# Seven products of quarters for the second matrix product of the last two token groups, with the activations' sums on GpSimd and on VectorE

## The chip, the cores and the metric

The kernel runs on one core of one Trainium2 chip. A core has TensorE (PE, which multiplies matrices from SBUF into PSUM), VectorE (DVE), ScalarE (ACT), GpSimd (POOL), and SyncE (SP), from whose queue most DMA transfers start. Each engine works through its own instructions in their order and waits on semaphores for the others. The metric is the device time of one execution in microseconds (us), lower is better.

## The reference

Attention in a causal window, then a two-layer MLP over its output:

```python
batch, n_heads, seq, head_dim = (8, 8, 576, 64)        # window = 128
scores = scale * np.matmul(q, k.transpose(0, 1, 3, 2))
scores = np.where(mask, scores + bias[None], -1000000000.0)   # mask: 0 <= rel < window
scores = scores - np.max(scores, axis=-1, keepdims=True)
attn = np.exp(scores)
attn = attn / (np.sum(attn, axis=-1, keepdims=True) + 1e-09)
attn_out = np.matmul(attn, v)
...
n_tokens, d_model, d_ff = (4608, 512, 2048)
x = attn_out.transpose(0, 2, 1, 3).reshape(B * S, H * D)
h = x @ w_in
g = h * (1.0 / (1.0 + np.exp(-h)))
return g @ w_out
```

## The kernel before

The 4608 tokens are nine groups of 512 (`NG` = 9, `TG` = 512), and the 2048 hidden columns are 16 blocks of 128 (`NF`). A *step* n = 16 g + f is group g with hidden block f: group 7 is steps 112 to 127, group 8 is steps 128 to 143. Every step has a first product (`gemm1`, line 650) into a PSUM bank `h`, an activation in four instructions, and a second product (`gemm2`, line 719) that adds into four PSUM banks `o` (tags w, x, y, z), one for each 128 tokens of the group.

From group 2 (first product) and 3 (second) on, all operands are float16 and each number is a high part and a low remainder; a product is high x high, high x low and low x high. So a step has 12 matmuls in the first product, 4 parts of the 512 inputs times 3, and 12 in the second, 4 tiles of tokens times 3, each of which moves 512 columns. In group 2 the first product has the same columns in 24 matmuls of 256.

The activation of a step: `act1` is a tanh on ScalarE from PSUM (line 666); `act2` on VectorE makes gt = (tanh + 1) h, with h from PSUM (671); `act3` on ScalarE rounds gt to the high part gh (681); `act4` on VectorE takes the remainder gl (687).

Attention for the later tokens runs among the MLP steps. It goes in 72 half blocks p: scores on TensorE (439), the bias with the row maximum on VectorE (469, four instructions), exp on ScalarE (479), a float16 high part on ScalarE (488) and remainder on VectorE (493), two DMA transposes, attention times v on TensorE (543), a division on VectorE (561, 562, 570) and a split of the result (580, 142). Ahead of a half block the float16 parts of q and k are made (385 on ScalarE, 391 on VectorE), and those of v once for two half blocks (415 on GpSimd, 421 on VectorE).

The order is written out by hand. The loop goes through positions, four for each step (two halves of `gemm1`, two halves of the `gemm2` of the step before), and a table `plan` says which other pieces are issued ahead of each position; within one position a small `rank` sorts them. An engine then runs what it was issued in that order. In group 7 a half block of attention falls on every second step: the scores stand ahead of the first product of an odd step, attention times v ahead of that of an even one. The last half block is issued before the end of group 7, and group 8 has no attention.

At the end of a group the second product of the last step follows at once on that of the step before it, so the activation of the last step has only one second product to hide behind.

## Time and profile before

| | |
|---|---|
| median of 3 runs | 926.47 us (925.91 to 926.49) |
| the profiled execution | 926.23 us, of which the traced span is 924.4 us |
| TensorE busy | 914.6 us (99%), granted clock 1.0 |
| VectorE / ScalarE / GpSimd busy | 645.0 / 559.6 / 116.0 us |
| group 7 (744.01 to 837.42 us of the span) | 93.41 us |
| group 8 up to the end of its matmuls (837.42 to 920.33 us) | 82.91 us |

In the rows of the profile a line number is that of the kernel before. `out<-in` are the program's names, `xN` counts instructions, and a time in brackets is how long the engine had been idle before the instruction, with what released it. Rows of the timeline give start and duration in us; a busy TensorE may still be a TensorE that overlaps the ends of its matmuls, so the pace of matmuls is read from their starts.

### The profile page before, as it was taken

The page shows a single profiled execution, that of the slowest core. Times are in us where ns is not written, and L with a number is a line of the kernel's source. Part 1 is how long each engine was busy: PE and PEld are TensorE (multiplying, and loading weights), DVE is VectorE, ACT ScalarE, POOL GpSimd, SP SyncE. Part 2 cuts the span into 40 slices and gives each one's busy share as a digit, 9 for nine tenths or more (in the row PEclk, how much of TensorE's full clock was granted, in tenths as well). Part 3 has the DMA queues.
Part 4 walks back from the last instruction along what each step waited for, and adds up shares of the span by engine and source line. Part 5 has one row for each costly group of instructions (what it writes and reads, how often), then busy time and mean ns, then how long its engine had stood idle before and what let it go on. Part 6 is the DMA issues. An engine that isn't in the chain of part 4 may idle for free.

```text
span 924.4 us, 17093 instructions
## 1 busy us (share of the span) xinstructions
PE 914.6 (99%) x6426; PEld 572.4 (62%) x6426; DVE 645.0 (70%) x1629; ACT 559.6 (61%) x1149; POOL 116.0 (13%) x115
## 2 busy tenths in 40 slices
PE   9999999999999999999999999999999999999998
PEld 8867777777787886555555555555555555544443
DVE  6889876446776778888788778666867777743222
ACT  7778997675556764666677755555655565533222
POOL 2343442222221220000000000000000000000000
PEclk9999999999999999999999999999999999999999
DMA  8977825243275645434598736444545454211001
GB/s 311 392 189 225 256 57 129 69 91 80 71 218 152 178 115 137 114 94 112 114 247 219 203 88 163 112 103 104 160 115 115 114 160 113 65 35 52 1 1 45
DMA packets 197747, 122.89 MB, mean 133 GB/s; under 512 B 166432, under 2 KB 166816, under 8 KB 197664
## 3 DMA queue, kind: packets, MB, share of 16 engines
q1 hardware_dynamic: 197376, 121.54, 49.3%
q8 instruction: 50, 0.82, 0.4%
q14 instruction: 33, 0.27, 0.1%
q10 hardware_dynamic: 288, 0.26, 0.1%
HBM read 71.96 MB, written 9.44 MB: 88 GB/s over the span
## 4 chain that ended last, share of the span: by engine, by line
PE 85%; DVE 5%; ACT 1%; issue 1%; ACTq 0%
PE o L719 38%; PE h L650 29%; PE h L655 8%; PE av L543 4%; PE sp L439 3%; PE sp L446 2%; DVE gt L671 1%; DVE hr L493 1%; DVE t L469 0%; DVE w L816 0%; DVE vmx L204 0%; ACT t L479 0%; DVE x L142 0%; ACT w L804 0%; DVE wr L810 0%
## 5 line engine op out<-in xcount | busy, mean ns | idle before, releaser
L719 PE MATMUL o<-w,gh 128*128 128x512 f16 (+1 forms) x1152 | 351.2, 386 | 0.0
L650 PE MATMUL h<-xt,w 128*128 128x512 f16 (+1 forms) x1536 | 310.5, 353 | 0.0
L650 PEld LDWEIGHTS <-w 128*128 128x128 f16 x1536 | 144.6, 98 | 125.8 <-issue 2.2
L666 ACT ACTIVATE gt<-h,gsc 128x512 f32<-128x512 f32 x112 | 77.0, 687 | 239.8 <-PE h L650 237.7
L719 PE MATMUL o<-w,gl 128*128 128x512 f16 (+1 forms) x576 | 221.6, 385 | 0.2 <-DVE gl L142 0.2
L671 DVE SCALAR_TENSOR_TENSOR gt<-gt,h 128x512 f32<-128x512 f32 x144 | 98.7, 686 | 147.3 <-ACT gt L666 146.8
L719 PEld LDWEIGHTS <-gh 128*128 128x128 f16 x768 | 74.8, 98 | 89.1
L479 ACT ACTIVATE t<-t,mx 128x256 f32<-128x256 f32 (+1 forms) x288 | 125.2, 486 | 5.2 <-DVE mx L469 5.0
L493 DVE SCALAR_TENSOR_TENSOR hr<-t,hr 128x512 f16<-128x512 f32 (+1 forms) x128 | 89.3, 703 | 29.7 <-ACT hr L488 29.6
L687 DVE SCALAR_TENSOR_TENSOR gl<-gt,gh 128x512 f16<-128x512 f32 x96 | 66.8, 696 | 42.4 <-ACT gh L681 41.3
L655 PE MATMUL h<-xh,w 128*128 128x512 f32 x256 | 89.8, 405 | 0.0
L719 PEld LDWEIGHTS o<-w,gh 128*128 128x128 f32 x384 | 69.8, 188 | 15.3 <-DVE vsc L264 0.3
L415 POOL TENSOR_SCALAR v<-rv,vsc 128x512 f16<-128x512 f32 x30 | 25.2, 841 | 427.8 <-DMA rv<-v 351.8
L681 ACT ACTIVATE gh<-gt 128x512 f16<-128x512 f32 x96 | 60.4, 629 | 28.1 <-DVE gt L671 23.7
L488 ACT ACTIVATE hr<-t 128x512 f16<-128x512 f32 (+1 forms) x128 | 71.4, 595 | 1.4 <-DVE hr L493 1.4
L719 PEld LDWEIGHTS <-gl 128*128 128x128 f16 x384 | 37.6, 98 | 46.2 <-DVE gl L687 1.2
L543 PEld LDWEIGHTS <-hl 128*128 128x128 f16 x1464 | 51.4, 98 | 16.5 <-issue 5.2
L469 DVE CUSTOM_DVE_ANT_0 t<-sp,tab,vsc 128x256 f32<-128x256 f32 (+1 forms) x144 | 58.5, 461 | 1.8 <-PE sp L439 1.4
L140 POOL TENSOR_TENSOR gl<-gt,gh 128x512 fp32r<-128x512 f32 x30 | 38.6, 1286 | 164.2 <-ACT gh L679 148.9
L543 PE MATMUL av<-v,hl 128*128 128x65 f16 (+1 forms) x1464 | 54.8, 193 | 1.6 <-DVE mx L469 1.5
L655 PEld LDWEIGHTS h<-xh,w 128*128 128x128 f32 x256 | 48.1, 188 | 12.3 <-issue 0.2
L469 DVE CUSTOM_DVE_ANT_0 t<-sp,tab 128x256 f32<-128x256 f32 (+1 forms) x144 | 50.1, 402 | 3.3 <-PE sp L446 2.9
(135 smaller groups left out, 1006.5 us busy)
## 6 DMA issues: line engine op xcount, KB each, us to landing
r<-qk SPq DMA_DIRECT2D x36, 512.0 KB, 3.9
qs<-qk SPq DMA_DIRECT2D x18, 512.0 KB, 5.1
out<-ot SPq DMA_DIRECT2D x35, 256.0 KB, 2.4
wr<-w_in SPq DMA_DIRECT2D x16, 512.0 KB, 6.7
wr<-w_out SPq DMA_DIRECT2D x16, 512.0 KB, 6.2
rv<-v SPq DMA_DIRECT2D x30, 256.0 KB, 4.0
vm<-v SPq DMA_DIRECT2D x27, 256.0 KB, 5.0
q<-qk SPq DMA_DIRECT2D x18, 256.0 KB, 3.3
```

Source lines behind the costliest of these rows:

```text
L469: nc.vector.tensor_tensor_reduce(out=st[p]["t"][u][:, h, 2 * P - n :], in0=st[p]["sp"][h][:, u, o].rearrange("p o c -> p (o c)"), in1=tab[ ...
L479: nc.scalar.activation(x, x, AF.Exp, bias=st[p]["mx"][:, 2 * u + h : 2 * u + h + 1], scale=-1.0)
L488: nc.scalar.activation(split_of(p, u, hr)[:, 0], t[:, :, 2 * P - n :], AF.Copy, scale=PSCALE)
L493: nc.vector.scalar_tensor_tensor(out=hr[:, 1], in0=t[:, :, 2 * P - n :], scalar=PSCALE, in1=hr[:, 0], op0=ALU.mult, op1=ALU.subtract)
L543: nc.tensor.matmul(av[:, 2 * u + h, : rhs.shape[-1]], lhs, rhs, start=(n == 0), stop=(n == len(seq) - 1), skip_group_check=True,)
L650: nc.tensor.matmul(o, w[:, wp, cc], x, start=start and k == 0, stop=stop, skip_group_check=True)
L655: nc.tensor.matmul(hps[n], w[:, cc], x, start=(half == 0 and i == 0), stop=(half == 1 and i == len(seq) - 1), skip_group_check=True,)
L666: nc.scalar.activation(gt, hps[n], AF.Tanh, scale=scale)
L671: nc.vector.scalar_tensor_tensor(out=gt, in0=gt, scalar=1.0, in1=hps[n], op0=ALU.add, op1=ALU.mult)
L681: nc.scalar.activation(gh, gt, AF.Copy, scale=CUT)
L687: nc.vector.scalar_tensor_tensor(out=gl, in0=gt, scalar=CUT, in1=gh, op0=ALU.mult, op1=ALU.subtract)
L719: nc.tensor.matmul(ops[ti], a[:, t], w, start=(f == 0 and i == 0), stop=(f == NF - 1 and i == len(seq) - 1), skip_group_check=True,)
```

## The change

Groups 7 and 8 (`FAST`) take a second product by quarters, seven instead of eight. A is the activation of 256 tokens (two tiles of 128) by two hidden blocks, j and j + 8; B is `w_out` of these two hidden blocks by two halves of 256 output columns. The seven products are (A11+A22)(B11+B22), (A21+A22)B11, A11(B12-B22), A22(B21-B11), (A11+A12)B22, (A21-A11)(B11+B12) and (A12-A22)(B21+B22); each moves 256 columns, again in three matmuls, and they are summed over j = 0 to 7 in halves of the banks w, x, y, z. Steps are renumbered within a group: the first eight are the first 256 tokens, the next eight the other 256, and a step's first product makes two hidden blocks for 256 tokens in 24 matmuls of 256 columns.

- `act_sums` makes the five sums of quarters of gt (two, two and one quarter, in three instructions), on GpSimd in group 7, on VectorE in group 8. `act3` and `act4` then work on seven quarters (one instruction of five, one of two) in place of four. In group 7 `act3` and `act4` are issued one position later than before.
- The float16 parts of the five sums of `w_out` are made in steps 80 to 111 (groups 5 and 6), for one j in every 16 positions (`SUM_WORK`): seven additions or subtractions and three instructions for remainders on GpSimd, four copies on ScalarE.
- v's high part moves from GpSimd to ScalarE in groups 7 and 8.
- After eight steps the seven products are joined on ScalarE (one instruction) and VectorE (six) and stored from there, three stores on SP's queue and one on ScalarE's. Behind a join the second product of the first step is issued one step later, so that it follows two first products.
- The very last step has its second product in the plain way, in quarters that are added and stored one by one.

On VectorE, at steps 116 to 118, before (t, mx: row maximum of half block 68; q16, k16: remainders for block 34; hr: remainder of the weights; r, xs: division; the rows `mx68` alone are left out):

```order
L671 SCALAR_TENSOR_TENSOR gt116_9778<-gt116_9778,h116_9757 128x512
L687 SCALAR_TENSOR_TENSOR gl116_9792<-gt116_9778,gh116_9791 128x512
L142 SCALAR_TENSOR_TENSOR x33_9795<-xs66_9767,x33_9795 128x256
L469 ISA t68_0_9831,mx68_9822<-sp68_0_9804,tab_65,vsc3_6995 128x256
...
L671 SCALAR_TENSOR_TENSOR gt117_9845<-gt117_9845,h117_9824 128x512
L391 SCALAR_TENSOR_TENSOR q16_69_9781<-r16_69_9636,vsc3_6995,q16_69_9781 64x512
L687 SCALAR_TENSOR_TENSOR gl117_9858<-gt117_9845,gh117_9857 128x512
L391 SCALAR_TENSOR_TENSOR k16_34_9679<-r16_69_9636,vsc3_6995,k16_34_9679 128x512
L493 SCALAR_TENSOR_TENSOR hr68_0_9863<-t68_0_9831,hr68_0_9863 128x512
...
L493 SCALAR_TENSOR_TENSOR hr68_1_9900<-t68_1_9833,hr68_1_9900 128x512
L671 SCALAR_TENSOR_TENSOR gt118_9923<-gt118_9923,h118_9902 128x512
```

and after:

```order
L763 SCALAR_TENSOR_TENSOR gt116_10026<-gt116_10026,h116_9991 128x512
L147 SCALAR_TENSOR_TENSOR x33_10048<-xs66_10007,x33_10048 128x256
L799 SCALAR_TENSOR_TENSOR gl116_10061<-gt116_10026,gh116_10060 128x640
L799 SCALAR_TENSOR_TENSOR gl116_10061<-gt116_10026,gh116_10060 128x256
L480 ISA t68_0_10099,mx68_10082<-sp68_0_10064,tab_65,vsc3_6996 128x256
...
L763 SCALAR_TENSOR_TENSOR gt117_10119<-gt117_10119,h117_10084 128x512
L399 SCALAR_TENSOR_TENSOR q16_69_10032<-r16_69_9839,vsc3_6996,q16_69_10032 64x512
L399 SCALAR_TENSOR_TENSOR k16_34_9889<-r16_69_9839,vsc3_6996,k16_34_9889 128x512
L504 SCALAR_TENSOR_TENSOR hr68_0_10142<-t68_0_10099,hr68_0_10142 128x512
...
L799 SCALAR_TENSOR_TENSOR gl117_10155<-gt117_10119,gh117_10154 128x640
L799 SCALAR_TENSOR_TENSOR gl117_10155<-gt117_10119,gh117_10154 128x256
L504 SCALAR_TENSOR_TENSOR hr68_1_10186<-t68_1_10101,hr68_1_10186 128x512
```

The remainder gl of the even step still stands ahead of the row maximum; that of the odd step now stands behind q16, k16, the first hr and the division. The three sums of each step stand on GpSimd, between gt here and gh on ScalarE.

On ScalarE, at the join in the middle of group 7 (step 120), after; `once` is the part of the join that ScalarE makes, `of` what is stored:

```order
L759 ACTIVATE gt120_10421<-h120_10386,gsc7_9586 128x512
L393 ACTIVATE q16_71_10427<-r16_71_10231,vsc3_6996 128x512
L884 ACTIVATE once7_0_10443<-m7_0_1_9798,gsc7_9586 128x512
L591 CAST x34_10447<-xs68_10402 128x256
L876 DMA out<-of7_0_0_10441 128x256
L784 ACTIVATE gh120_10467<-gt120_10421 128x640
L784 ACTIVATE gh120_10467<-gt120_10421 128x256
L393 ACTIVATE k16_35_10282<-r16_71_10231,vsc3_6996 128x512
L759 ACTIVATE gt121_10526<-h121_10491,gsc7_9586 128x512
```

The store's DMA stands ahead of gh of step 120 and of the tanh of step 121; before, there was no store at this place.

The diff, cut to its core:

```diff
+FAST = (NG - 2, NG - 1)
+HALF_F = NF // 2
+SUMS, SUMS_STEP = 320, 16
...
     def v_hi(i):
         rv = rvs[i]
+        if pos[0] // (SLICE * NF) in FAST:
+            nc.scalar.activation(v1[:, i % VSLOTS, :, 0:D], rv, AF.Copy, scale=vsc[i // NBLK][:, 0:1])
+            return
...
+    def sum_float(j, k):
+        if k == 0:
+            wsum["r"] = pool.tile([P, 2, DM], F32, tag="big", name=f"wr{j}")
+        w = w16[1, j + k * HALF_F]
+        nc.gpsimd.tensor_add(wsum["r"][:, k], w[:, 0], w[:, 1])
+
+    def sum_make(j, k):
...
+        if k == 0:
+            nc.gpsimd.tensor_sub(q[:, 0], b12, b22)
+            nc.gpsimd.tensor_sub(q[:, 1], b21, b11)
+        elif k == 1:
+            nc.gpsimd.tensor_add(q[:, 2], b11, b22)
+            nc.gpsimd.tensor_add(q[:, 3], b21, b22)
+        else:
+            nc.gpsimd.tensor_add(b11, b11, b12)
...
+    def gemm1_fast(n, half):
+        g, (t, j) = n // NF, divmod(n % NF, HALF_F)
+        w = w16[0, j + HALF_F * (1 - half)]
+        out = hps[n][:, half * TG // 2 : (half + 1) * TG // 2].rearrange("p (t c) -> p t c", t=2)
+        seq = [(wp, xp, cc) for cc in range(NCC) for wp, xp in ((0, 0), (0, 1), (1, 0))]
...
+    def parts_of(n):
+        return [(slice(0, 4), slice(0, 4))] if n == LAST else [(slice(2, 7), slice(3, 8)), (slice(0, 2), slice(1, 3))]
...
+    def act_sums(n):
+        if n == LAST:
+            return
+        engine, a = nc.vector if n // NF == NG - 1 else nc.gpsimd, gact[n]
+        pairs = a[:, 0:4].rearrange("p (a b) c -> p a b c", b=2)
+        engine.tensor_add(a[:, 4:6], a[:, 2:4], a[:, 0:2])
+        engine.tensor_sub(a[:, 6:8], pairs[:, :, 0], pairs[:, :, 1])
+        engine.tensor_add(a[:, 3], a[:, 2], a[:, 1])
...
+            for to, of in parts_of(n):
+                nc.scalar.activation(gh[:, to], gt[:, of], AF.Copy, scale=0.5 * CUT)
...
+    def gemm2_fast(n, half):
...
+        products = (M5, M2, M1, M3) if half == 0 else (M4, M7, M6)
+        for a, parts in ((gh, (0, 1)), (gl, (0,))):
+            for k in products:
...
+                for part in parts:
+                    nc.tensor.matmul(
+                        product(k), a[:, k], sum_part(k, j, part),
...
+        if n == last:
+            join_products(g, t, half)
...
+    def gemm2_last(half):
...
+        for col, o in ((0, product(M7)), (1, c)) if half == 0 else ((0, c), (1, product(M6))):
...
+            add_product(o, st["out"][0 if half == col else 1][:, half], NG - 1)
+            store_fast(NG - 1, 1, half, col)
...
+        (nc.scalar if row and col else nc.sync).dma_start(rows, st["out"][0 if row == col else 1][:, row])
+
+    def join_products(g, t, half):
...
+            nc.scalar.activation(once.rearrange("p a c -> p (a c)"), ops[1], AF.Copy, scale=scale)
+            for k in range(2):
+                nc.vector.scalar_tensor_tensor(
+                    out=st["out"][0][:, k], in0=product(M1), scalar=scale, in1=once[:, k], op0=ALU.mult, op1=ALU.subtract
+                )
+            return
...
+    SUM_WORK = (
+        [(sum_float, 0)], [(sum_float, 1)], [(sum_make, 0)], [(sum_make, 1)], [(sum_make, 2), (sum_hi, 0)],
+        [(sum_hi, 1), (sum_lo, 0)], [(sum_hi, 2)], [(sum_lo, 1)], [(sum_lo, 2)],
+    )
...
+                behind = [n - 1] if f or g - 1 in FAST else []
+                if g in FAST and f in (1, 2, HALF_F + 1, HALF_F + 2):
+                    behind = [] if f % HALF_F == 1 else [n - 2, n - 1]
+                if g == NG - 1 and f >= NF - 2:
+                    behind = [] if f == NF - 2 else [n - 2, n - 1, n]
...
+                        elif n // NF in FAST and n // NF < NG - 1:
+                            ahead(4, act4, n)
+                            ahead(3, act3, n)
+                            ahead(1, act_sums, n)
+                            ahead(1, act2, n)
```

More of the change, by code (lines that the diff above doesn't have):

```diff
@@ L66 @@
 CUT = 2.0**-25
+FAST = (NG - 2, NG - 1)
+HALF_F = NF // 2
+SUMS, SUMS_STEP = 320, 16
+SUM_TAGS = tuple(f"w1_{k}" for k in range(7, 15))
+MORE_TAGS = (("w1_15", 1), ("k", KSLOTS), ("k", KSLOTS))
 STATS, CONV_IN, CONV_OUT = 66, 106, 172
@@ new lines, in sum_lo @@
+    def sum_lo(j, k):
+        if k < 2:
+            out16, a = wsum[0, j][:, 2 * k : 2 * k + 2], wsum["q"][:, 2 * k : 2 * k + 2]
+            nc.gpsimd.tensor_sub(out16[:, :, 1], a, out16[:, :, 0])
+            return
+        out16 = wsum[1, j]
+        nc.gpsimd.tensor_sub(out16[:, 1], wsum["r"][:, 0, : DM // 2], out16[:, 0])
+    def gemm1_fast(n, half):
[3 more added lines that the diff above has]
+        seq = [(wp, xp, cc) for cc in range(NCC) for wp, xp in ((0, 0), (0, 1), (1, 0))]
+        for i, (wp, xp, cc) in enumerate(seq):
+            nc.tensor.matmul(
+                out, w[:, wp, cc], xt[g, "g"][:, 2 * t : 2 * t + 2, xp * NCC + cc],
+                start=half == 0 and i == 0, stop=i == len(seq) - 1, skip_group_check=True,
+            )
@@ L704, in turn_over @@
                 x_parts(i + k, 1)
+    def gemm2_fast(n, half):
+        g, (t, j) = n // NF, divmod(n % NF, HALF_F)
+        last = LAST - 1 if n // HALF_F == LAST // HALF_F else n - j + HALF_F - 1
+        if n == LAST:
+            gemm2_last(half)
+            return
+        gh, gl, _ = gact[n]
+        products = (M5, M2, M1, M3) if half == 0 else (M4, M7, M6)
+        for a, parts in ((gh, (0, 1)), (gl, (0,))):
+            for k in products:
+                b, side = PLACE[k]
+                if j == 0 and side == 0 and a is gh:
+                    ops[b] = psum.tile([P, DM], F32, tag="wxyz"[b], name=f"m{g}_{t}_{b}")
+                for part in parts:
+                    nc.tensor.matmul(
+                        product(k), a[:, k], sum_part(k, j, part),
+                        start=j == 0 and side == 0 and a is gh and part == 0, stop=n == last and a is gl,
+                        skip_group_check=True,
+                    )
+        if n == last:
+            join_products(g, t, half)
@@ new lines, in product @@
+    def product(k):
+        b, side = PLACE[k]
+        return ops[b][:, side * (DM // 2) : (side + 1) * (DM // 2)]
+    def gemm2_last(half):
+        gh, gl, _ = gact[LAST]
+        if half == 0:
+            ops["c"] = ps_of("a", "last")
+        c = ops["c"][:, half * (DM // 2) : (half + 1) * (DM // 2)]
+        for col, o in ((0, product(M7)), (1, c)) if half == 0 else ((0, c), (1, product(M6))):
+            seq = [
+                (a[:, k], w16[1, HALF_F - 1 + far * HALF_F][:, part, col * (DM // 2) : (col + 1) * (DM // 2)])
+                for k, far in ((2 + half, 0), (half, 1)) for a, part in ((gh, 0), (gh, 1), (gl, 0))
+            ]
+            for i, (lhs, rhs) in enumerate(seq):
+                nc.tensor.matmul(
+                    o, lhs, rhs, start=half == 0 and col == 1 and i == 0, stop=i == len(seq) - 1, skip_group_check=True
+                )
+            add_product(o, st["out"][0 if half == col else 1][:, half], NG - 1)
+            store_fast(NG - 1, 1, half, col)
@@ new lines, in add_product, with store_fast @@
+    def add_product(m, o, g):
+        nc.vector.scalar_tensor_tensor(out=o, in0=m, scalar=gsc[g][:, 2:3], in1=o, op0=ALU.mult, op1=ALU.add)
+    def store_fast(g, t, row, col):
+        first = g * TG + (2 * t + row) * P
+        rows = out[first : first + P, col * (DM // 2) : (col + 1) * (DM // 2)]
+        (nc.scalar if row and col else nc.sync).dma_start(rows, st["out"][0 if row == col else 1][:, row])
+    def join_products(g, t, half):
+        scale = gsc[g][:, 2:3]
+        if half == 0:
+            st["out"] = [pool.tile([P, 2, DM // 2], F32, tag="q", bufs=2, name=f"of{g}_{t}_{k}") for k in range(2)]
+            st["once"] = once = pool.tile([P, 2, DM // 2], F32, tag="io", name=f"once{g}_{t}")
+            nc.scalar.activation(once.rearrange("p a c -> p (a c)"), ops[1], AF.Copy, scale=scale)
+            for k in range(2):
+                nc.vector.scalar_tensor_tensor(
+                    out=st["out"][0][:, k], in0=product(M1), scalar=scale, in1=once[:, k], op0=ALU.mult, op1=ALU.subtract
+                )
+            return
+        (corner, other), once = st["out"], st["once"]
+        nc.vector.scalar_tensor_tensor(
+            out=other, in0=ops[0].rearrange("p (a c) -> p a c", a=2), scalar=scale, in1=once, op0=ALU.mult, op1=ALU.add
+        )
+        for k, m in enumerate((M4, M3)):
+            add_product(product(m), corner[:, k], g)
+        if n_last(g, t):
+            return
+        nc.vector.scalar_tensor_tensor(
+            out=corner, in0=ops[2].rearrange("p (a c) -> p a c", a=2), scalar=scale, in1=corner, op0=ALU.mult, op1=ALU.add
+        )
+        for row in range(2):
+            for col in range(2):
+                store_fast(g, t, row, col)
@@ L706, in gemm2, with n_last @@
+    def n_last(g, t):
+        return g == NG - 1 and t == 1
     def gemm2(n, half):
         g, f = divmod(n, NF)
+        if g in FAST:
+            gemm2_fast(n, half)
+            return
         for ti in (2 * half, 2 * half + 1):
@@ L896, in tile_window_attention_then_silu_mlp @@
         put(STATS + k, w_stat, k % 2, k // 2)
+    for j in range(HALF_F):
+        n = SUMS + SUMS_STEP * j
+        for k, work in enumerate(SUM_WORK):
+            for fn, part in work:
+                put(n + k, fn, j, part)
     for x, wait in enumerate((0, 2, 5)):
```

73 lines of the change are left out of this document (63 added, 10 removed).

## The prediction

> **What bounds the kernel now.** I read the table of busy time first, then the waits of TensorE, then the two last groups by stretches of time, then the timeline of one stretch.
>
> ```profile
> PE 914.6 (99%) x6426; PEld 572.4 (62%) x6426; DVE 645.0 (70%) x1629; ACT 559.6 (61%) x1149; POOL 116.0 (13%) x115
> PEld L719 <- DVE gl L687: 1.2, 3, 0.4
> 744.01:837.42 93.41, 93.41 (x649) 47.90 (x648) 59.29 (x143) 46.69 (x89) 2.60 (x3) 1.00 0.39 95
> 837.42:920.33 82.91, 82.91 (x384) 37.23 (x382) 23.60 (x34) 22.27 (x35) 0.00 (x0) 1.00 0.03 13
> ```
>
> The second row is all that TensorE waited for from 545 us on: 1.2 us in three places. The others are groups 7 and 8 (length, then busy time of PE, its weight loads, DVE, ACT, POOL, then the clock, 1.00). TensorE has work without a gap, so matmuls that go are time that goes, as long as the activations still arrive in time. GpSimd is nearly free there (2.60 us of 93.41).
>
> **What TensorE saves.**
>
> ```profile
> 881.38 2.75 PE L650 MATMUL h<-xt,w 128*128 128x512 f16 x12
> 883.97 0.59 PE L719 MATMUL o<-w,gh 128*128 128x512 f16 x2
> ...
> 313.11 2.79 PE L650 MATMUL h<-xt,w 128*128 128x256 f16 x24
> 315.66 0.71 PE L719 MATMUL o<-w,gh 128*128 128x512 f32 x2
> ...
> 318.51 1.48 PE L650 MATMUL h<-xt,w 128*128 128x256 f16 x12
> 319.83 0.34 PE L543 MATMUL av<-v,hl 128*128 128x65 f16 x6
> ```
>
> Twelve matmuls of 512 columns go from 881.38 to 883.97: 2.59 us, 0.216 each. With 256 columns, and a weight load for each, 24 take 2.55 (0.106; the float32 matmul behind them is recorded early) and 12 take 1.32 (0.110). I take 0.109. The change's matmuls have this form.
>
> - Second product, group 7: 192 x 0.216 = 41.44 becomes 2 x 7 x 8 x 3 = 336 x 0.109 = 36.62, a saving of 4.82. In group 8 the last step keeps 24 of the plain kind in place of 21: 339 x 0.109 = 36.95, a saving of 4.49.
> - First product: 24 x 0.109 = 2.62 in place of 2.59, in 32 steps: 0.96 lost.
>
> Together -8.35 us (-12.8 at 0.106, -7.0 at 0.110).
>
> **The end.**
>
> ```profile
> 918.16 0.10 PEld L719 LDWEIGHTS <-gl 128*128 128x128 f16 x1 [0.42 <-DVE gl L687]
> 920.12 0.38 PE L719 MATMUL o<-w,gl 128*128 128x512 f16 x1
> 920.53 0.47 ACT L730 ACTIVATE ot<-o,gsc 128x256 f32<-128x256 f32 x1
> 921.04 0.48 DVE L731 TENSOR_SCALAR ot<-o,gsc 128x256 f32<-128x256 f32 x1 [1.05 <-ACT ot L730]
> 921.55 0.33 SPq L733 DMA_DIRECT2D out<-ot  x1
> ```
>
> The wait of 0.42 goes, since the last second product now has two others ahead of it (4.6 us). Behind the last matmul VectorE stood idle until ScalarE was done; now it adds quarters (0.48 each) as they come, with a small queue from the join: I take 0.25 less, between 0 and 0.5. Together -0.65.
>
> **What the activations now take in group 7.** One pair of steps before, even and odd, ScalarE first:
>
> ```profile
> 768.00 0.69 ACT L666 ACTIVATE gt<-h,gsc 128x512 f32<-128x512 f32 x1 [1.99 <-PE h L650]
> 774.07 0.69 ACT L666 ACTIVATE gt<-h,gsc 128x512 f32<-128x512 f32 x1 [3.08 <-PE h L650]
> 776.85 1.13 ACT L488 ACTIVATE hr<-t 128x512 f16<-128x512 f32 x2
> ...
> 767.80 0.59 PE L719 MATMUL o<-w,gh 128*128 128x512 f16 x2
> 779.77 0.59 PE L719 MATMUL o<-w,gh 128*128 128x512 f16 x2
> ...
> 768.72 0.69 DVE L671 SCALAR_TENSOR_TENSOR gt<-gt,h 128x512 f32<-128x512 f32 x1 [1.10 <-ACT gt L666]
> 770.11 0.69 DVE L687 SCALAR_TENSOR_TENSOR gl<-gt,gh 128x512 f16<-128x512 f32 x1 [0.70 <-ACT gh L681]
> 770.72 0.42 DVE L142 SCALAR_TENSOR_TENSOR x<-xs,x 128x256 f16<-128x256 f32 x1
> 771.37 0.48 DVE L469 CUSTOM_DVE_ANT_0 t<-sp,tab,vsc 128x256 f32<-128x256 f32 x1 [0.24 <-PE sp L439]
> 774.80 0.69 DVE L671 SCALAR_TENSOR_TENSOR gt<-gt,h 128x512 f32<-128x512 f32 x1 [1.72 <-ACT gt L666]
> 776.30 0.69 DVE L687 SCALAR_TENSOR_TENSOR gl<-gt,gh 128x512 f16<-128x512 f32 x1
> 776.91 0.75 DVE L391 SCALAR_TENSOR_TENSOR k<-r,vsc,k 128x512 f16<-128x512 f32 x1
> 777.57 0.68 DVE L493 SCALAR_TENSOR_TENSOR hr<-t,hr 128x512 f16<-128x512 f32 x1
> ```
>
> A pair takes TensorE 779.77 - 767.80 = 11.97 us; after the change 11.97 - 4 x 2.59 + 2 x 2.62 + 2 x 2.29 (21 x 0.109) = 11.43. Before, gl of the odd step was done at 776.99 and needed from 779.77 on, with 2.8 us to spare; and the row maximum (771.37) was done before the next tanh (774.07).
>
> GpSimd's sums have no row of their own size. The price of gh for four quarters, the nearest row to a sum, and a sign of what stands in the sums' way:
>
> ```profile
> L681 ACT ACTIVATE gh<-gt 128x512 f16<-128x512 f32 x96 | 60.4, 629 | 28.1 <-DVE gt L671 23.7
> L140 POOL TENSOR_TENSOR gl<-gt,gh 128x512 fp32r<-128x512 f32 x30 | 38.6, 1286 | 164.2 <-ACT gh L679 148.9 <-issue 15.3
> ...
> 753.07 0.76 DVE L391 SCALAR_TENSOR_TENSOR k<-r,vsc,k 128x512 f16<-128x512 f32 x1
> 753.11 1.20 POOL L415 TENSOR_SCALAR v<-rv,vsc 128x512 f16<-128x512 f32 x1 [26.61 <-PE av L543]
> 753.76 1.09 DVE L493 SCALAR_TENSOR_TENSOR hr<-t,hr 128x512 f16<-128x512 f32 x1
> ...
> 796.14 0.48 DVE L469 CUSTOM_DVE_ANT_0 t<-sp,tab,vsc 128x256 f32<-128x256 f32 x1
> 796.15 0.70 POOL L415 TENSOR_SCALAR v<-rv,vsc 128x512 f16<-128x512 f32 x1 [21.61 <-DMA rv<-v]
> ```
>
> By 1286 ns for 512 columns, two sums of 256 and one of 128 take 1.6 by their size; with some 0.05 an instruction I take 1.75 (bounds 1.6 and 2.0). They don't run beside everything: the same GpSimd instruction takes 0.70 beside a row maximum (one operand in PSUM), but 1.20 when it meets VectorE's k (two operands in SBUF), and VectorE's hr behind it ends at 754.85, 0.54 after GpSimd's end, in place of 0.68 after its start. So the two engines take turns, some 0.55 for VectorE's share, as long as VectorE reads two operands from SBUF: q, k, hr, x, v and gl do, gt and the row maximum don't.
>
> Now the order. VectorE has the even step's gl ahead of the row maximum, and that of the odd step's gt behind it; ScalarE has the next tanh behind the odd step's gh and the copy of hr. So the odd gt waits for the row maximum, that for the even gl, that for the even sums, those for the even gt, that for the tanh, and the tanh for the odd gh, which waits for the odd sums. This is a loop of VectorE, GpSimd and ScalarE that goes round once in a pair, whatever TensorE does:
>
> - odd gt 0.69; the three sums 1.75 between q, k and hr, 3 x 0.55: 3.3 with a small overlap; hand-over and gh of five quarters 0.8 (629 ns for four, some 0.1 for a fifth);
> - on ScalarE the rest of gh 0.31, the copy of hr 0.54 (half of 1.13), the next tanh 0.69, less overlap: 1.45; even gt with a wait for hr's second remainder 0.95;
> - sums 1.75 + x 0.3 + hand-overs, 2.2, and in every other pair v, 2.75; gh 0.8; gl of five and two quarters 1.1; row maximum 4 x 0.4 = 1.6; back to the odd gt.
>
> The sum is 12.9, and 13.45 with v: 13.2 in the mean against TensorE's 11.43. From the odd gt of step 113 to that of step 123 it goes round five times: 5 x 1.77 = 8.9 us in which TensorE waits. I choose this over no waiting since both engines show the turns at this very place in group 7. The join at step 120 comes on top: on VectorE six more instructions (0.36 for a half and 0.61 for a whole bank, 2.7), and the store's DMA (0.35) that ScalarE must issue before gh of step 120. GpSimd's sums cover part; gh comes 2.1 later. So TensorE waits 11.0 in group 7 (bounds: none, if the sums never met VectorE, and 14).
>
> One page prices the sums otherwise: the Trainium skill, GPSIMD Engine Reference, section 3.1, has 4497 ns for a two-input float32 add of 2048 elements, by which 640 elements are an estimated 1.4 us. This case's row is dearer, 2.5 ns a column. By the page's figure the loop would be 0.7 shorter, and the total 3.5 us lower.
>
> **Joins in group 8.** VectorE makes the sums itself (0.42, 0.42, 0.3; no GpSimd in the way), and a step needs about 4.4 us to its gl, while two products and a bit, 5.8, lie ahead. Only at a join is it late: ScalarE's DMA waits for the last of the join, 6.8 us after the first product of step 128; then DMA 0.35, tanh, gt, sums and gh of step 129 (0.69 + 0.69 + 1.15 + 0.74 and hand-overs) end at 10.6, and TensorE is there at 2.29 + 2 x 2.62 + 2.29 = 9.82. Steps 129 and 137: 2 x 0.75 = 1.5 (bounds 0 and 3).
>
> **Edits costed at nothing.** The sums of w_out in groups 5 and 6, by 1286 ns for 512 columns some 9 us of GpSimd and four copies on ScalarE for every j, eight times: a step's gl has about 3 us to spare, as above, which covers two turns of 1.3; with that cover gone they cost up to 1 us each. v's high part on ScalarE stands ahead of an even step's gh, which waits for GpSimd anyway. Three of a join's stores stand on SP's queue ahead of the transposes of half block 70 and of the next load of v; both are used a pair of steps later, 11 us, while a join takes 4.
>
> **The sum** against the profiled execution's 926.23 (span 924.4): -8.35 - 0.65 + 11.0 + 1.5 = +3.5. The profiled time lies 0.24 under the median, so I forecast 930.0 by the runs' median of 926.47.
>
> **The rivals.**
>
> - *The sums fit in (faster).* If GpSimd's short sums seldom meet VectorE, the loop is 13.2 - 3 x 0.55 - 0.3 - 0.3 = 10.95, under 11.43, and TensorE waits only at step 113 (0.9: act4 behind the division), at the join of step 120 (2.0) and for group 8's 1.5: 926.47 - 9.0 + 4.4 = 921.9. For it: 0.70 in the row of 796.15. Against it: three of them stand just where VectorE has q, k and hr. It decides from a loop under 11.43.
> - *All of it is hidden (faster)*: also no waiting at joins, 917.5. Against it: DMA behind VectorE on ScalarE's queue.
> - *The sums of w_out stall groups 5 and 6 (slower still).* From about 3 us of GpSimd between gt and gl on, the second product waits; a burst of five to seven sums could bring four turns of up to 1.3. At 1 us for each of eight: 938. Against it: a burst is followed by a long pause.
>
> **How the numbers follow.** Forecast 0.55, the sums fit in 0.27, all hidden 0.08, groups 5 and 6 stall 0.10. A measurement here tells about 0.2% (1.9 us) from no change. The forecast's own range is 925.5 to 934.5: slower 0.43 of its 0.55, same 0.11, faster 0.01; the fit gives faster 0.22 and same 0.05. Faster 0.31, same 0.16, slower 0.53. The range that holds 8 in 10 is 920 to 935.
>
> **What would show it.** Starts of 256-column matmuls 0.109 apart in both products. In the waits of TensorE, some 9 to 11 us on gh and gl of odd steps in group 7, and 0.7 at steps 129 and 137. GpSimd's sums of 256 over 1 us long where VectorE has q, k or hr, and 0.65 else. If group 7 is under 93 us, the loop is wrong; if groups 5 and 6 together grow, that cover was.

## The result, and the profile after

The changed kernel takes 936.93 us in the median of 4 runs (933.99 to 938.60), the kernel before 926.48 beside it: a ratio of 1.0112, 95% interval 1.0099 to 1.0124. The forecast was 930.0, in a range of 920 to 935: slower as forecast, by three times as much. The profiled execution took 936.24 us (span 934.5 us, mean granted clock 0.998), 10.0 more than that of before.

By stretches, from the starts of TensorE's products in both traces (step 112's first product starts at 743.84 before and 747.44 after; step 127's second product ends at 837.26 and 850.11, and after has 2.62 of the first product of 128 within; step 143's first product ends at 915.05 and 922.10; 2.29 of second product now stands behind that point and not ahead of it):

| stretch | forecast | measured |
|---|---|---|
| up to group 7 | 0 | +3.60 |
| group 7 | -4.82 + 0.48 + 11.0 = +6.66 | +6.63 |
| group 8 to the end of step 143's first product | -14 x 0.30 + 0.48 + 1.5 = -2.2 | -0.9 |
| from there to the end | -0.65 - 0.27 = -0.9 | +0.7 |
| sum | +3.5 | +10.0 |

The waits of TensorE in the changed kernel (who waited for whom: total us, times, longest):

```profile
PE m L839 <- ACT gh L784: 6.0, 5, 1.7
PE m L839 <- DVE gl L799: 3.0, 4, 1.6
PE av L554 <- DVE mx L480: 2.1, 3, 0.8
PE sp L450 <- DVE vsc L300: 1.8, 1, 1.8
PE last L863 <- DVE of L870: 1.4, 1, 1.4
PE vs L298 <- DVE r L572: 1.3, 1, 1.3
```

The first two are the forecast waits for gh and gl. Those with `vs` and `last` are new, the one with `vsc` was 0.5 before, and nothing in the forecast stands for them. (The one with `mx` was 1.5 before.)

**Entry of group 5.** GpSimd and VectorE after, then VectorE before, at the same work:

```profile
535.88 2.72 POOL L654 TENSOR_TENSOR wr<-w 128x512 f32<-128x512 f16 x2
538.67 1.06 POOL L663 TENSOR_TENSOR wq<-wr 128x256 f32<-128x256 f32 x1
...
537.69 1.45 DVE L804 SCALAR_TENSOR_TENSOR gl<-gt,gh 128x512 f16<-128x512 f32 x1
539.07 1.21 DVE L399 SCALAR_TENSOR_TENSOR k<-r,vsc,k 128x512 f16<-128x512 f32 x1
540.20 1.21 DVE L504 SCALAR_TENSOR_TENSOR hr<-t,hr 128x512 f16<-128x512 f32 x1
542.10 0.60 DVE L288 TENSOR_SCALAR row<-row 1x3 f32<-1x3 f32 x1
547.51 0.15 DVE L300 COPY vsc<-vs 128x8 f32<-128x8 f32 x1
```

```profile
537.03 0.68 DVE L687 SCALAR_TENSOR_TENSOR gl<-gt,gh 128x512 f16<-128x512 f32 x1
537.63 0.74 DVE L391 SCALAR_TENSOR_TENSOR k<-r,vsc,k 128x512 f16<-128x512 f32 x1
538.29 0.68 DVE L493 SCALAR_TENSOR_TENSOR hr<-t,hr 128x512 f16<-128x512 f32 x1
539.66 0.16 DVE L283 TENSOR_SCALAR row<-row 1x3 f32<-1x3 f32 x1
544.32 0.16 DVE L295 COPY vsc<-vs 128x8 f32<-128x8 f32 x1
```

The first sums of w_out are issued with step 80, whose first product starts at 557.00, but GpSimd has nothing ahead of them and starts them at 535.88, as soon as a v is done. There VectorE makes the scale of the next pair of sequences (`row`, `vsc`), for which the next scores wait. Its instructions wait for GpSimd's, even one of three elements (0.60 for 0.16); `vsc` comes at 547.51 in place of 544.32. Of the 3.60 us ahead of group 7, 2.64 come up here and 0.4 in the steps up to 96.

**Joins and end.** The rows of ScalarE, VectorE and TensorE at the join of step 120, at that of step 128 and in the last step:

```profile
804.21 0.75 DVE L898 SCALAR_TENSOR_TENSOR of<-m,gsc,of 128x512 f32<-128x512 f32 x1
804.99 0.38 ACTq L876 DMA_DIRECT2D out<-of  x1
805.41 1.04 ACT L784 ACTIVATE gh<-gt 128x640 f16<-128x640 f32 x2 [3.78 <-DVE of L898]
...
813.19 0.61 PE L839 MATMUL m<-w,gh 128*128 128x256 f16 x4 [1.72 <-ACT gh L784]
815.26 0.61 PE L839 MATMUL m<-w,gl 128*128 128x256 f16 x2 [1.02 <-DVE gl L799]
...
856.08 0.69 ACT L759 ACTIVATE gt<-h,gsc 128x512 f32<-128x512 f32 x1 [3.69 <-DVE of L898]
859.43 0.61 PE L839 MATMUL m<-w,gh 128*128 128x256 f16 x4 [1.62 <-ACT gh L784]
...
929.56 0.38 PE L863 MATMUL last<-w,gh 128*128 128x256 f16 x2 [1.40 <-DVE of L870]
```

Behind a join ScalarE stands 3.7 us behind its store, which waits for VectorE's last instruction (L898). In the last step the second half of the product goes into the other half of the same PSUM tile and waits until VectorE has read the first half.

### The profile page after: what moved, and what is told of

It reads as the page before. It is cut to its first block, busy times and chain, and to the rows that moved or that the text cites. A ratio compares the mean times of both kernels' runs of the same rounds, so it can differ in the third digit from the quotient of the medians.

```text
span 934.5 us, 18785 instructions
## 1 busy us (share of the span) xinstructions
PE 910.6 (97%) x7101; PEld 637.4 (68%) x7101; DVE 717.3 (77%) x1731; ACT 587.5 (63%) x1214; POOL 235.9 (25%) x240
## 4 chain that ended last, share of the span: by engine, by line
PE 74%; DVE 12%; ACT 3%; issue 2%; POOL 1%; ACTq 0%; POOLq 0%; DVEq 0%
PE o L924 28%; PE h L732 20%; PE h L737 8%; PE h L704 5%; PE m L839 4%; PE av L554 4%; PE sp L450 3%; PE sp L457 2%; DVE gt L763 2%; DVE gl L799 2%; DVE hr L504 1%; DVE t L480 1%; ACT gt L759 1%; DVE q L399 1%; DVE k L399 1%
## 5 line engine op out<-in xcount | busy, mean ns | idle before, releaser
L924 PE MATMUL o<-w,gh 128*128 128x512 f16 (+1 forms) x896 | 275.3, 389 | 0.3 <-ACT gh L790 0.3
L732 PE MATMUL h<-xt,w 128*128 128x512 f16 (+1 forms) x1152 | 222.6, 344 | 0.0
L924 PE MATMUL o<-w,gl 128*128 128x512 f16 (+1 forms) x448 | 173.0, 386 | 0.3
L732 PEld LDWEIGHTS <-w 128*128 128x128 f16 x1152 | 107.7, 98 | 83.6 <-issue 2.2
L924 PEld LDWEIGHTS <-gh 128*128 128x128 f16 x512 | 49.7, 98 | 59.2
L704 PE MATMUL h<-xt,w 128*128 128x256 f16 x768 | 88.3, 273 | 0.0
L924 PEld LDWEIGHTS o<-w,gh 128*128 128x128 f32 x384 | 69.8, 188 | 15.9 <-ACT gh L790 0.8
L704 PEld LDWEIGHTS <-w 128*128 128x128 f16 x768 | 74.6, 98 | 8.7
L804 DVE SCALAR_TENSOR_TENSOR gl<-gt,gh 128x512 f16<-128x512 f32 x64 | 55.0, 859 | 25.6 <-ACT gh L792 24.8
L784 ACT ACTIVATE gh<-gt 128x640 f16<-128x640 f32 (+2 forms) x63 | 32.9, 569 | 59.3 <-POOL gt L776 27.5
L799 DVE SCALAR_TENSOR_TENSOR gl<-gt,gh 128x640 f16<-128x640 f32 (+2 forms) x63 | 38.8, 655 | 25.9 <-ACT gh L784 25.9
L145 POOL TENSOR_TENSOR w<-wm,w 128x512 fp32r<-128x512 f32 x32 | 43.3, 1355 | 59.3 <-ACT w L981 59.0
```

Of the source, the lines that this page charges most:

```text
L145: engine.tensor_sub(out, a, b)
L704: nc.tensor.matmul(out, w[:, wp, cc], xt[g, "g"][:, 2 * t : 2 * t + 2, xp * NCC + cc], start=half == 0 and i == 0, stop=i == len(seq) - 1, ...
L732: nc.tensor.matmul(o, w[:, wp, cc], x, start=start and k == 0, stop=stop, skip_group_check=True)
L924: nc.tensor.matmul(ops[ti], a[:, t], w, start=(f == 0 and i == 0), stop=(f == NF - 1 and i == len(seq) - 1), skip_group_check=True,)
```

## The experiments

The kernel before is timed beside each; its median was 926.1 to 926.4. Differences inside a run are read from its trace, since the starts of the kernels differ by up to 1.2 us (below) and the lowered clock moves them by more (last section).

### The parts one by one

**VectorE's sums.** The sums of group 7 on VectorE:

```diff
-        engine, a = nc.vector if n // NF == NG - 1 else nc.gpsimd, gact[n]
+        engine, a = nc.vector, gact[n]
```

> The activations' sums of group 7 move from GpSimd to VectorE, as group 8 has them; nothing else. Theory (GpSimd and VectorE take turns, and the loop of VectorE, GpSimd and ScalarE sets group 7's pace): the sums then cost VectorE 1.15 us a step with no turns, the loop of a pair falls from 13.2 to about 13.2 - (3.3 - 1.15) - (2.35 - 1.15) = 9.85 us, below TensorE's 11.43; only the joins' delays stay, and group 7 falls from 97.4 to 92 to 94 us: 932 to 933 in all. Rival (VectorE alone is the bound there, since it has 59.3 us of work in group 7 before, and gets 7.5 of wider gl): 18 us more of work on it make 85 of 91 us, and with its order it is late more often: 937 or more.

934.55 us (933.13 to 937.14), ratio 1.0094 [1.0077, 1.0111]. Group 7 takes 99.74 us against 100.05: nearly nothing, though the pairs from step 115 to 121 run at 11.4 to 11.7 us, as forecast. The time now goes at the start of each half of the group: the second products of 112 and 113 take 8.70 together in place of 4.58, those of 120 and 121 8.51. So group 7 has a second cause besides the loop.

**Group 8 alone.**

```diff
-FAST = (NG - 2, NG - 1)
+FAST = (NG - 1,)
```

> Only the last group has the seven products; group 7 is computed as in the kernel before (with v's high part back on GpSimd), the sums of w_out are made as in the change. Theory (group 7's stalls are its loop): group 7 goes back to its 90.8 us and the stay of the clock at full speed with it: 936.9 - 6.6 = 930.3. Rival (the stalls are not group 7's own but follow from work that the sums of w_out or a later layout pushed there): group 7 stays near 97 us and the time near 937, less nothing.

927.29 us (926.80 to 927.98), ratio 1.0011 [1.0002, 1.0020]. Group 7 is back to its old pace (its last step starts 3.3 us later than before, its first too). It gained 3 us more than I had expected: with group 7 goes its second join too, and so the 1.8 us that step 129 waited, and the lowered clock; and the run starts 0.5 us nearer to the kernel before. All the rest stays: the waits for `vs`, `vsc` and `last` are there with 1.5, 1.8 and 1.4 us.

**Later sums of w_out.**

```diff
-SUMS, SUMS_STEP = 320, 16
+SUMS, SUMS_STEP = 336, 14
```

> The sums of w_out begin at place 336 in place of 320, every 14 places in place of 16; so GpSimd has the next v's high part, which it does not start before 564 us, ahead of the first sum. Theory (the first sums, which GpSimd started at 535.9 us, slowed VectorE's chain to the second batch's scale, for which the scores wait): that chain takes 7.2 us again in place of 10.0, the two waits of 1.8 and 1.3 us at about 546 us go, and the time falls by 2.65 to about 934.3. Rival (the loss at the entry of group 5 has another cause, or the sums stall elsewhere by as much as soon as they are moved): 936.9.

933.85 us (932.32 to 934.66), ratio 1.0081 [1.0066, 1.0096]: 3.1 less. GpSimd and VectorE:

```profile
563.09 1.24 POOL L426 TENSOR_SCALAR v<-rv,vsc 128x512 f16<-128x512 f32 x1 [28.05 <-DMA rv<-v]
564.29 2.71 POOL L654 TENSOR_TENSOR wr<-w 128x512 f32<-128x512 f16 x2
...
537.02 0.75 DVE L399 SCALAR_TENSOR_TENSOR k<-r,vsc,k 128x512 f16<-128x512 f32 x1
543.71 0.16 DVE L300 COPY vsc<-vs 128x8 f32<-128x8 f32 x1
```

The sums now start at 564.29 and nothing meets the chain to `vsc`, and steps 80 and 112 start at the same distance from the kernel before as step 8 does. So the 3.05 us are shown to come from where the first sums fall: in their new places all eight sets cost nothing.

The remaining 0.55 us ahead of group 7 arise by step 4. The kernels of this study, with the same work up to 535 us, stand there at -0.6 to +0.57 from the kernel before, so it is not the change.

**Two tiles in the last step.**

```diff
-        if half == 0:
-            ops["c"] = ps_of("a", "last")
-        c = ops["c"][:, half * (DM // 2) : (half + 1) * (DM // 2)]
+        c = ps_of("a", f"last{half}")[:, half * (DM // 2) : (half + 1) * (DM // 2)]
...
-                    o, lhs, rhs, start=half == 0 and col == 1 and i == 0, ...
+                    o, lhs, rhs, start=half != col and i == 0, ...
```

> The two halves of the last step's own product go to two PSUM tiles in place of two halves of one. Theory (the second half's matmuls wait for VectorE to have read the first half, since both lie in one tile): the wait of 1.40 us at 929.6 goes; VectorE then has its adds one behind the other and ends about 1.15 us earlier: 936.9 - 1.15 = 935.8, and the span from the last step's first matmul to the end shrinks by 1.15. Rival (the matmuls wait for VectorE's queue in another way, or the stores set the end): no change, 936.9.

934.78 us (934.62 to 936.25), ratio 1.0098 [1.0082, 1.0115]. By the traces, from the tanh of step 143 to the end it is 1.02 us shorter. VectorE and TensorE:

```profile
927.27 1.26 DVE L868 SCALAR_TENSOR_TENSOR of<-m,gsc,of 128x256 f32<-128x256 f32 x3
...
928.58 0.38 PE L861 MATMUL m<-w,gh 128*128 128x256 f16 x2 [0.35 <-DVE of L868]
```

TensorE does not wait for the first half any more; a wait of 0.35 stays, of the same kind (bank y: VectorE reads its one half, for M7, up to 928.53, and the matmuls that add to M6 in the other half start at 928.58).

**The joins' stores on SP's queue.**

```diff
-        (nc.scalar if row and col else nc.sync).dma_start(rows, ...)
+        (nc.scalar if row and col and n_last(g, t) else nc.sync).dma_start(rows, ...)
```

> The fourth store of the joins of steps 120, 128 and 136 is issued from SP's queue, with the other three, and no longer from ScalarE's (the last join keeps its own). Theory (in that queue the store waits for VectorE's last instruction of the join, and gh of step 120 and the tanh of steps 129 and 137 wait behind it): ScalarE's idle 3.8 us ahead of that store at 805 us goes, gl of step 120 waits for VectorE's join alone and the two stalls of TensorE around step 121 (4.4 and about 0.7) shrink to 2 or less together; the stalls at steps 129 and 137 (1.8 and 1.1) go: 5 to 6 us less, about 931. Rival (the join's six instructions on VectorE are what is late, and the store only stands beside them): 1 us less or none, 936 to 937. Rival (SP's queue now holds back the transposes behind the stores): another stall comes up in the steps after 121.

932.58 us (932.49 to 933.31), ratio 1.0064 [1.0047, 1.0081]: 4.4 less. In group 8 the second products behind the joins take 5.09 and 4.58 in place of 6.38 and 5.68, so 2.4 of 2.9 us came from the store. Around step 121 little was won:

```profile
803.91 1.05 ACT L784 ACTIVATE gh<-gt 128x640 f16<-128x640 f32 x2 [1.63 <-POOL gt L776]
...
813.41 0.61 PE L839 MATMUL m<-w,gh 128*128 128x256 f16 x4 [2.34 <-ACT gh L784]
```

gh of step 120 comes 1.5 us earlier (1.1 within the group), but TensorE waits for gh of step 121 all the same. The second products of 120 and 121 still take 8.83 together, in place of 8.99. From the first product of 121 to that of 123 it is 15.9 us in place of 16.8, and the pairs ahead are 0.6 longer: group 7 takes 99.76. So the store was the cause in group 8, and only a small part in group 7. (Of the 4.4, 2.4 are the joins', 0.4 lies ahead of group 7 and 0.3 in it; the rest is the end and the spread of the medians.)

**The order at step 112.**

```diff
-                            ahead(4, act4, n)
-                            ahead(3, act3, n)
+                            first = n % NF == 0
+                            if first:
+                                later(2, act4_first, n)
+                            else:
+                                ahead(4, act4, n)
+                            ahead(2 if first else 3, act3, n)
```

`act4_first` is act4 under a name that the sorting within a place leaves behind the row maximum.

> In the first step of group 7 alone (step 112), gh is put ahead of the next tanh on ScalarE, and gl ahead of the next gt on VectorE. Theory (the first steps of that group have no second product between them, so four places of the order are two steps there, and gl of 112 stands behind the work of step 113): the wait of 2.8 us at the second product of 112 shrinks to 0.3 or less: 2.5 us less, about 934.4. Rival (the loop of VectorE, GpSimd and ScalarE sets the pace from there on, and gl of 113 or a later step is late by what is won): no change, 936.9.

936.34 us (934.82 to 937.10), ratio 1.0103 [1.0088, 1.0118]. The second products of 112 and 113 take 6.71 in place of 7.36, and group 7 99.17: less was to be won at 112 than I had expected. In the change's own trace the second product of 112 takes 2.7 us, and that of 113 4.65: most of the 2.8 us was a wait for gl of 113, not of 112. Here they take 2.3 and 4.4, and TensorE waits for gh of 113. TensorE in the change's trace, then here, and here GpSimd's sums of step 113, with VectorE's k beside them:

```profile
762.57 0.39 PE L839 MATMUL m<-w,gl 128*128 128x256 f16 x2 [1.60 <-DVE gl L799]
...
760.18 0.61 PE L842 MATMUL m<-w,gh 128*128 128x256 f16 x4 [1.27 <-ACT gh L784]
...
756.00 1.29 POOL L774 TENSOR_TENSOR gt<-gt 128x256 f32<-128x256 f32 x1 [2.64 <-DVE gt L763]
757.26 1.17 POOL L775 TENSOR_TENSOR gt<-gt 128x256 f32<-128x256 f32 x1
758.51 0.84 POOL L776 TENSOR_TENSOR gt<-gt 128x128 f32<-128x128 f32 x1
...
756.72 1.12 DVE L399 SCALAR_TENSOR_TENSOR k<-r,vsc,k 128x512 f16<-128x512 f32 x1
```

The three sums take 3.35 us where they meet q, k and hr, as in the forecast's loop (3.3); those of step 112, free, take 0.73, 0.73 and 0.45. Here they make gh of 113 late. In the change's own order they take 2.87, and what is late there is gl of 113, which VectorE has behind gt of step 114, hr and the division.

### Several together

**All mended, sums on VectorE.** The edits above together (VectorE's sums, later sums of w_out, two tiles, SP's queue, step 112).

> All mendings at once: the sums of group 7 on VectorE, the sums of w_out from place 336 on, two tiles for the last step, the joins' stores on SP's queue, and the order of step 112. Theory (the causes are separate places, and each gives back its own): from the 934.5 of the run with VectorE's sums, less 3.0 (entry of group 5), 1.0 (end), 4.1 (step 112), 4.5 (step 120) and 2.9 (the joins of group 8): 919. Rival (with all sums VectorE is the bound of group 7, and what is won at one place is lost at the next): 925 or more.

928.18 us (926.45 to 929.28), ratio 1.0017 [1.0008, 1.0027], 9 more than expected. The entry of group 5, the end and the joins of group 8 gave back their parts; group 7 still takes 100.86. TensorE waits twice for gl, 5.8 us in all: for gl of 113 and of 121. In VectorE's order this stands behind gt and sums of the next step, hr and the division. Behind both waits the clock is lowered (last section): the second products of both pairs and the scores and first product behind them take 11.1 us more than where nothing waits, and only 5.8 of these were waited.

**Group 8 alone, mended.**

```diff
-FAST = (NG - 2, NG - 1)
+FAST = (NG - 1,)
-SUMS, SUMS_STEP = 320, 16
+SUMS, SUMS_STEP = 336, 14
```

and the two tiles and SP's queue as above.

> The seven products in the last group alone, with the sums of w_out from place 336 on, two tiles for the last step and the joins' stores on SP's queue. Theory: from the 927.3 of the run with the last group alone, less 3.0 (entry of group 5), 1.0 (end) and 2.9 (joins): 920.4. Rival (group 8 cannot give back its joins, since VectorE's queue and not the store holds the next step): 922 to 924.

922.22 us (922.10 to 922.35), ratio 0.9953 [0.9938, 0.9967]: faster than the kernel before. In the trace the second products behind the join take 4.58 in place of 5.68: no wait at all. The measured time is 1.8 above the expectation, which had counted 2.9 for two joins; with group 7 in the old way there is one, with 1.1.

**The order of steps 113 and 121.** On top of the run with all mended and VectorE's sums, gh of these steps ahead of the next tanh, gl ahead of the next gt:

```diff
-                            first = n % NF == 0
-                            if first:
+                            first, second = n % NF == 0, n % HALF_F == 1
+                            if second:
+                                later(2, act3_first, n)
+                            if first or second:
                                 later(2, act4_first, n)
...
```

> All mendings of the run with VectorE's sums, and in steps 113 and 121 too, the second of each half of group 7, gh stands ahead of the next tanh and gl ahead of the next gt. Theory (in that run gl of 113 and 121 stood behind the next step's gt and sums and the division by the attention's sums, while the second product of 113 and 121 follows directly on that of 112 and 120; that is the whole of the two stalls of 3.9 and 5.2 us that were left): both go, and the clock stays at 1.00: 928.2 - 9.1 - about 1 of the lower clock = 918. Rival (VectorE has no time there, and what goes first pushes the rest by as much): 925 or more.

922.86 us (922.45 to 923.03), ratio 0.9963 [0.9949, 0.9977]: 5.3 less, and the clock stays at 1.00. Group 7 falls from 100.86 to 93.99; the second products of 112 and 113 take 4.59. Not all of the 9.1 came: the next scores now wait for the division (`xs`), which this order puts later on VectorE:

```profile
PE sp L450 <- DVE xs L581: 2.9, 2, 1.7
```

**The same with GpSimd's sums.** The only difference to the run before is the engine of group 7's sums.

> The same with the sums of group 7 left on GpSimd, as in the change; so the difference from the run before it is GpSimd against VectorE, with nothing else in the way. Theory of the prediction (the loop takes 13.2 us a pair with GpSimd's sums and 9.85 with VectorE's, against 11.43 for TensorE): 8.9 us above it, 927. The loop with the size seen in the change's trace (stalls of 0.8 and 1.7 in two pairs of four): 3 to 5 above it, 921 to 923. Rival (once the order is right the sums fit in): the same, 918.

929.12 us (927.47 to 930.00), ratio 1.0030 [1.0021, 1.0040]: 6.3 more than with VectorE's sums. Group 7 takes 98.75 against 93.99. From one odd step's first product to the next (115, 117, 119, 121) it is 13.5, 12.7 and 13.1 us, with VectorE's sums 11.4, 11.6 and 11.7. The loop was forecast at 13.2 against TensorE's 11.43.

**GpSimd's sums in the even steps alone.** On top of the run before, the odd steps' sums on VectorE:

```diff
-        engine, a = nc.vector if n // NF == NG - 1 else nc.gpsimd, gact[n]
+        engine, a = nc.vector if n // NF == NG - 1 or n % 2 else nc.gpsimd, gact[n]
```

> The same with the sums of the odd steps on VectorE and of the even steps on GpSimd. Theory (only the odd steps' sums meet q, k and hr, the even ones x and every other time v): the loop is 13.2 - 2.15 = 11.05 us, under 11.43, so no pair is late: as with all on VectorE, 918, with less work on VectorE. Rival (GpSimd's sums cost the loop by their own length, not by meeting VectorE): half of what all on GpSimd cost, 920 or more.

923.84 us (923.12 to 923.99), ratio 0.9971 [0.9960, 0.9982]. In total only 1.0 above VectorE's sums, but by the pairs (13.3, 12.6, 13.0) my theory fell: without any sum beside q, k and hr the loop is as long as before. (The three pairs cost 4.2 us; 3.1 come back at the starts of the halves, where VectorE is spared the sums of 112, 114, 120 and 122.) Two pairs of VectorE in groups (busy us, mean ns, then idle time ahead and its cause), with all sums on GpSimd, then with the even ones alone:

```profile
L799 DVE SCALAR_TENSOR_TENSOR gl<-gt,gh 128x640 f16<-128x640 f32 (+1 forms) x8 | 4.6, 620 | 4.5 <-ACT gh L784 4.5
L504 DVE SCALAR_TENSOR_TENSOR hr<-t,hr 128x512 f16<-128x512 f32 x4 | 3.2, 812 | 0.0
L399 DVE SCALAR_TENSOR_TENSOR q<-r,vsc,q 64x512 f16<-64x512 f32 x2 | 2.6, 1324 | 0.1
L399 DVE SCALAR_TENSOR_TENSOR k<-r,vsc,k 128x512 f16<-128x512 f32 x2 | 2.2, 1118 | 0.0
```

```profile
L799 DVE SCALAR_TENSOR_TENSOR gl<-gt,gh 128x640 f16<-128x640 f32 (+1 forms) x8 | 4.6, 620 | 4.5 <-ACT gh L784 4.5
L504 DVE SCALAR_TENSOR_TENSOR hr<-t,hr 128x512 f16<-128x512 f32 x4 | 2.7, 685 | 0.0
L399 DVE SCALAR_TENSOR_TENSOR k<-r,vsc,k 128x512 f16<-128x512 f32 x2 | 1.5, 752 | 0.0
L399 DVE SCALAR_TENSOR_TENSOR q<-r,vsc,q 64x512 f16<-64x512 f32 x2 | 1.5, 752 | 0.1
```

The turns cost VectorE 1.2 us a pair (0.57 at q, 0.37 at k, 2 x 0.13 at hr), and the odd step's sums, made by VectorE itself, cost it 1.14 (0.43 + 0.42 + 0.29): no difference. What makes the pair long in both is the idle time ahead of gl, 2.25 us a pair: VectorE has gl of the even step ahead of the row maximum and stands still until GpSimd's sums and gh are there. With all sums on VectorE the same row has 0.5 in two pairs, and the pairs take 11.4 to 11.7. (The counterpart, the odd steps' sums alone on GpSimd, was not run.)

**The division first.** On top of the run with the order of 113 and 121 and VectorE's sums, gt and sums of steps 114 and 122 behind the division:

```diff
-                            ahead(1, act_sums, n)
-                            ahead(1, act2, n)
+                            third = n % HALF_F == 2
+                            ahead(2 if third else 1, act_sums, n)
+                            ahead(2 if third else 1, act2, n)
```

> As the run with VectorE's sums and the mended order of steps 113 and 121; now gt and the sums of steps 114 and 122 stand behind the division by the attention's sums on VectorE, not ahead of it. Theory (in that run the next scores waited 1.4 and 1.9 us at 758 and 807 us for the division, which stood behind gt and three sums, 1.8 us): both waits go, 922.9 - 3.3 = 919.6. Rival (VectorE is full there, and gh or gl of 114 and 122 is late instead): 922 to 923.

921.79 us (921.30 to 922.60), ratio 0.9954 [0.9941, 0.9968], the lowest of the study and level with group 8 alone, mended. The waits for the division are gone (scores at 0.89 and 1.03 in place of 2.29 and 2.75), but gl of step 115 is now late by 1.9:

```profile
PE m L845 <- DVE gl L799: 2.2, 2, 1.7
```

So 1.1 of 3.3 us came. Two pairs of the run with the order of 113 and 121 and VectorE's sums (stretch, length, then busy time of PE, weight loads, VectorE, ScalarE, GpSimd, clock) show why: VectorE is busy for 10.85 of 11.57 and 11.45 of 11.70 us, and has hardly any time left to move.

```profile
771.79:783.36 11.57, 11.57 (x133) 10.27 (x131) 10.85 (x29) 8.14 (x16) 0.00 (x0) 1.00 0.39 114
783.36:795.06 11.70, 11.63 (x134) 10.27 (x132) 11.45 (x30) 8.30 (x16) 0.00 (x0) 1.00 0.52 114
```

## Why the prediction was right or wrong

**What TensorE saves**: right. 24 matmuls of 256 columns take 2.62 us and 21 take 2.29 wherever nothing waits.

**Edits costed at nothing**: the step that failed most. The sums of w_out were put at nothing and cost 3.05 us, nearly half of the 6.5 by which the traces exceed the forecast's +3.5 (1.6 more are the end, 1.3 group 8, and 0.55 the start, which varies). I had the right cover (3 us at a step's gl) for the wrong place: I read the sums where the program issues them, in steps 80 to 111, and looked there for gl. GpSimd, with nothing ahead of them, starts the first set 21 us ahead of step 80's first product, beside a chain on VectorE with no cover. The rival "the sums of w_out stall groups 5 and 6" named the right work, but as 1 us in each of eight sets; 2.64 of it are in the first. No wait of TensorE names v's high part on ScalarE, but no run changed it alone.

**The end**: wrong by 1.6 (forecast -0.9 with its share of the saving, measured +0.7). The working counted VectorE's adds of quarters and overlooked that two of them share a PSUM tile with matmuls still to come; 1.02 of it came back with two tiles.

**Joins in group 8**: right in mechanism and place (ScalarE's store behind the join), 2.9 instead of 1.5. My 0.75 a join took the chain up to gh; measured are 1.8 and 1.1, and without the store 0.5 and 0.

**Group 7**: the sum of 11.0 was met (11.05: 2.8 at 112 and 113, 2.9 at 117 and 119, 5.4 around 121), but not for the reasons given; that it agrees is luck. The loop, forecast at 13.2 us a pair, runs at 12.7 and 13.1 in the two pairs in which it shows, and at 13.1 in the mean once the order is mended; but it was to be late five times, 8.9 us, and is so by 2.9. The starts of the two halves, for which the forecast had 2.1 at a join (and 0.9 at step 113 only in a rival), take 8.2. There two second products follow each other (at step 112 too, where no join lies ahead), while gl of the second stands behind the next step's work in VectorE's order (at 121 TensorE waits 1.72 for gh first, then 1.02 for gl, and the lowered clock takes about 1.6). The two causes hide each other: either mended alone wins 0.3 to 1.3 us of group 7's 100.05, no more than these times vary, both together 6.

| group 7, us | the change's order | order of 112, 113, 121 mended |
|---|---|---|
| GpSimd's sums | 100.05 | 98.75 |
| VectorE's sums | 99.74 | 93.99 |

(Mended, the store stands on SP's queue too, which alone gives 99.76. Each entry on the left holds one fall of the clock, at most 1.7 us, and those on the right none. With the clock such times vary by 1 to 2.6 us: 102.62 in the run with the later sums, which has two falls.)

Why the loop is long was half right. That GpSimd and VectorE take turns is shown (q 1324 ns for 752, sums 3.35 us for 1.9), but moving the odd sums away does not shorten the loop, since made on VectorE they cost it as much as the turns. Moving the even ones too does, and with them goes VectorE's idle time ahead of gl. So the forecast's parts (3.3 for the odd sums, 2.35 for the even) made up the right sum, but taking away the turns at q, k and hr, which it blamed most, does not bring the pair under TensorE's.

**GpSimd's price**: 0.72, 0.72 and 0.45, or 1.9 us for a step's sums where nothing meets them, above my 1.75 and within its bounds. The estimate of 1.4 from the figure in the Trainium skill (GPSIMD Engine Reference, section 3.1) would have been too low.

**The rivals**: "the sums fit in" is refuted by the pairs of 12.7 to 13.5 us with GpSimd's sums, and the 6.3 us between GpSimd's and VectorE's sums. "All of it is hidden" is not reached by any version: the best gains 4.4 of the 9.0.

## What to carry to other kernels

An engine without work ahead of an added piece starts it as soon as its inputs allow, not where the program issues it: look in the trace where it stands idle, and what chain runs there on the engine it hinders. Where a schedule counts positions, look for the steps that have fewer of them (here the first two of each half) and follow each engine's order there by itself. A late order and a long loop hide each other, so take both away before calling either harmless; and a mended part (here group 8) may be worth as much as the whole.
